# Two pairs of heads in four 64x64 quadrants: products of batch 0 and batch 1 laid out crossed

## The chip, the cores and the metric

The kernel runs on one NeuronCore of a Trainium2 chip. Its engines work side by side and wait for each other by semaphores: TensorE (PE, with its weight loads shown as PEld), VectorE (DVE), ScalarE (ACT), GpSimd (POOL) and SyncE (SP); transfers between the chip's main memory and on-chip memory (SBUF) are made by DMA engines. The results of TensorE stand in PSUM, an accumulator memory that is handed out in banks of 128 partitions x 512 float32. The metric is the time on the device in microseconds (us) of one execution, the median of several runs.

## The reference

q, k and v have shape (8 batches, 8 heads, 576 tokens, 64). Heads 0 to 3 are plain: a token attends to itself and the 31 tokens before it. Heads 4 to 7 are dilated: every fourth token, 32 of them. The result goes through a two-layer network with a squared ReLU.

```python
scores = scale * np.matmul(q, k.transpose(0, 1, 3, 2))
rel = pos[:, None] - pos[None, :]
mask_plain = (rel >= 0) & (rel < window)                                   # window = 32
mask_dil = (rel >= 0) & (rel < window * dilation) & (rel % dilation == 0)  # dilation = 4
attn = np.exp(scores - max); attn = attn / (np.sum(attn, axis=-1, keepdims=True) + 1e-09)
attn_out = np.matmul(attn, v)                                              # (8, 8, 576, 64)
x = attn_out.transpose(0, 2, 1, 3).reshape(8 * 576, 512)
h = np.maximum(x @ w_in, 0.0)                                              # w_in 512 x 2048
out = h * h @ w_out                                                        # w_out 2048 x 512
```

## The kernel before

**Pairs of heads.** Two heads of 64 features share the 128 partitions: pair e = 0, 1 is plain, e = 2, 3 dilated. Head 0 of a pair has the partitions 0 to 63, head 1 has 64 to 127 ("sides"). Keys are cut into blocks of 64. Scores stand with keys on partitions and queries along the row (`pt`, in bfloat16, after the exponential and the mask). The product with v needs, for each block, a weight tile of 128x128 that has head 0's v in the upper left 64x64 and head 1's in the lower right, with zeros elsewhere (`vbd`, and `kbd` likewise for k). Sums over the keys come from the same rows with a tile of ones in the same two corners. So a plain pair's product is a row of matmuls with 128x128 weights that use half of the array.

**Batches.** Batch 0 is the start of the kernel and has its own code (`first_step`); batch 1 goes through `trans`, `halves`, `scores` and `pv`; batches 2 to 7 through `quadrants` (L661), where two pairs are computed at once in four 64x64 quadrants of the array. For this one of the two pairs is "crossed" (`crossed`): its heads' k, v and scores are laid out with the sides exchanged, so that its weights stand in the two corners which the other pair leaves free. Batches 0 and 1 are computed in two parts, part 0 with the first 256 tokens, part 1 with the other 320.

**Steps.** The order of the attention work is written out by hand in the string PROGRAM. A bar separates the FFN's groups: after the group with number g the steps behind the bar number g + 1 are issued. Every engine takes its instructions in the order in which they were issued. In batch 0 a step has a letter, a pair and a part: T and C transpose and copy out, S makes scores, E is the exponential and the mask, P the products, D the sums, L the logarithm of the sums, X the exponential of its negative (so the reciprocal), M the product of both, into `xT`, the FFN's input. Steps of batch 1 begin with 1: q, k (Q, K for part 1) transposes, a (b) scores with exponential and mask, o (p) products, sums, reciprocal and the write to `xT`. A step with an f takes its PSUM from the pool `ps_f`, which the FFN uses too. j copies rows of v of batch 0 into `vbd`, and n zeroes `kbd` for batch 1.

**FFN.** A group computes 2 to 8 matmuls of the first layer (L937, evicted by ACT's ReLU and squared on DVE) or 4 of the second (L979). The first 1024 tokens go through it 256 at a time, the others 512 at a time. The group that first needs part 1 of pairs 0 and 1 of batch 0 comes two groups after P11 and D11.

The lines that matter here: `pv` has the products at L414 and the sums at L416, ACT's L418 and L419, and the write to `xT` on DVE at L429. In `first_step` the same are L851 (P), L867 (D), L874 (L), L877 (X) and L884 (M); masks are at L362 and L824. In batch 0:

```python
P01 D01 L01 X01 M01 P11 D11 L11 X11 M11     # after the fifth FFN group
```

Of the kernel before, what the change touches and what calls it, by code (L numbers as in the profile page):

```python
# [12 lines left out]
RES = 4  # L13
# [9 lines left out]
    "L1:q00123 z y L1:v0dp L1:q10123 w10 T00 C00a T10 C10a B00 B10 w1 S00 E00 B20 W1 S10 E10 N u B30 W1 w1 T20q "  # L23
    "w1 T20k C20v T30 C30v h W1 w1 S20 E20 w1 S30 E30 T21 C21v T31 C31a G20 G30 P00 P10 D00 D10 L00 X00 P20 P30 "
    "D20 D30 L20 X20 M00 j S21 S31 w1+31 M20 E21 E31 G21 G31a | | T01 C01v T11 C11a R P21 P31 D21 D31 S01 S11 L21 "
    "X21 M21 L31 X31 M31 E01 E11 | L2:q00123 L2:q10123 L1:v1dpr | | P01 D01 L01 X01 M01 P11 D11 L11 X11 M11 | | | "
    "| | | | | | | | | m n | | | | | | 1q1 1q3 | 1q2f 1k2f | 1k1a 1v3 | 1a2 | 1v2 1k0a 1q0v | 1o2 | 1a0 1a1 | 1k3 "
    "1o0 1o1f | 1a3 1Q0 | 1K0 1o3 | 1Q1 1K1 | 1Q2 | 1b0 | | 1Q3 1K2 L2:vwp L3:q00123 L3:q10123 L2:vwdr | L2:x | | "
    "| | 1V2 | 1b2 1p0 | 1b1 1V3 1K3 | L3:x | 1p2 1p1f | 1b3 | 2t0 2t1 1p3f | | | L3:Vd0 L4:q00123 L4:q10123 "
    "L3:V1 | | | | | | | | | | L4:x | | f | | | | | | | | | | | | | | | | L4:Vd L5:q10123 L5:q00123 L4:V01 | | | "  # L30
    "| | | | | | | | | | | | | L5:x | L5:Vd L6:q10123 L6:q00123 L5:V01"
)
# [30 lines left out]
def kernel(  # L63
# [9 lines left out]
    nc = tc.nc  # L73
# [100 lines left out]

    def crossed(b: int, e: int):

        return int(b == XB and e in (1, 3) or b >= NATURAL and e == 1 or b >= PAIRED and e == 0)

    def load_v(b: int, parts, which="pdr"):

# [85 lines left out]
    def trans(b: int, e: int, nm: str, part: int, home: str):  # L266

        pool, name = (ps_f, "pf") if "f" in home else (ps_a, "pa")
        ps = pool.tile([P, 1024], bf16, name=name)
        t = staged(b, nm)  # L270
        copy = copier(nm, e, home)
        m0, n, pitch, cuts = MS[part], MN[part], 80, [(t[0 : MT[part], part, :, :], 0, MT[part])]
        pv_ = ps[:, 0 : 4 * pitch].rearrange("p (h c m) -> p h c m", h=2, c=2)
        for hl in range(2):
            for c in range(2):
                for src, c0, w in cuts:
                    nc.tensor.transpose(  # L277
                        pv_[:, hl, c, c0 : c0 + w], src[:, 2 * e + hl, P * c : P * c + P], ident[0:w, 0:w]
                    )
        ready[b, e, nm] = pv_[:, :, :, 0:n], m0, n, copy  # L280
        halves(e, nm, *ready[b, e, nm], (0,) if "l" in home else (0, 1))

    ready = {}

# [1 line left out]
        act = "a" in home or "v" not in home and nm == "q" and e < NE // 2  # L286
        return nc.scalar.copy if act else nc.vector.tensor_copy

    def halves(e: int, nm: str, t, m0: int, n: int, copy, his=(0, 1)):


        for hl in his:
            rows = slice(64 * hl, 64 * hl + 64)
            for jj in range(2):
                src = t[64 * jj : 64 * jj + 64, hl, :, :]
                if nm == "q":
                    copy(
                        qT[rows, e, :, m0 : m0 + n].rearrange("p (c j) m -> p j c m", j=2)[:, jj, :, :], src
                    )
                elif e < NE // 2:  # L300
                    copy(
                        kbd[rows, e, m0 // 16 : (m0 + n) // 16, rows].rearrange(
                            "p i (m c j) -> p j i m c", c=2, j=2)[:, jj, :, :, :],
                        src.rearrange("p c (i m) -> p i m c", m=16),
                    )
                else:
                    x0, x1 = m0 // 64, min((m0 + n) // 64, 2)
                    copy(
                        kbd[rows, e, RES * x0 : RES * x1, rows].rearrange(
                            "p (x c j) m -> p j c x m", c=2, j=2)[:, jj, :, :, :],  # L310
                        src[:, :, 0 : 64 * (x1 - x0)].rearrange("p c (x m) -> p c x m", m=64),
                    )
                    if m0 + n == M:
                        copy(
                            kbd[rows, e, 8, rows].rearrange("p (m c j) -> p j m c", c=2, j=2)[:, jj, :, :],
                            src[:, :, n - 16 : n].rearrange("p c m -> p m c"),
                        )
# [46 lines left out]
            in1=mask[:, off : off + n], op=ALU.mult,  # L364
        )

    def pv(b: int, e: int, part: int, spare=None, name=""):
        dil = e >= NE // 2
        pt, vb = pts[e], vbd[b % 2]
        if spare is None:  # L370
# [20 lines left out]
        else:  # L391
# [9 lines left out]
            for i, r, m0, m1 in () if mms else blocks(b, e, part):  # L401
# [8 lines left out]
                    w = m1 - m0  # L410
                    mms.append((o3[:, r, x0:x1], i, pt[:, c : c + w]))
                c += w
        for x, (oo, i, rh) in enumerate(mms):
            nc.tensor.matmul(oo, vb[:, e, i, :], rh, start=(x == 0), stop=(x == len(mms) - 1), skip_group_check=True)  # L414
        for x, (dd, rh) in enumerate(dms):
            nc.tensor.matmul(dd, ones[:, :], rh, start=(x == 0), stop=(x == len(dms) - 1), skip_group_check=True)  # L416
        rec = r_pool.tile([P, 576], f32, name="rec")
        nc.scalar.activation(rec[:, 0:n], d[:, 0:n], ACT.Ln)  # L418
        nc.scalar.activation(rec[:, 0:n], rec[:, 0:n], ACT.Exp, scale=-1.0)  # L419
# [13 lines left out]
    def step(b: int, code: str):  # L433

        what, e, home = code[0], int(code[1]), code[2:]
        part = int(what in "QKVbp")
        his = (0,) if "l" in home else (1,) if "h" in home else (0, 1)
        if what in "qk" and (b > XB or b == XB and e >= NE // 2):  # L440
            t = (qx if what == "q" else kx)[b % 2]
            halves(e, what, t[:, 2 * e : 2 * e + 2, :, :], 0, M, copier(what, e, home), his)
        elif what in "qQkK" and "h" in home:
            halves(e, what.lower(), *ready[b, e, what.lower()], his)
        elif what == "t":
            trans_both(e)
        elif what in "qQkK":
            trans(b, e, what.lower(), part, home)
        elif what in "vV":
            spread_v(b, e, [part] if b in PARTED else [0, 1])  # L450
        elif what in "ab":
            scores(b, e, part)
        elif "f" in home:
            pv(b, e, part, ps_f, "pf")
        else:
            pv(b, e, part)
# [278 lines left out]
    def first_step(code: str):  # L735
# [56 lines left out]
        elif what == "S":  # L792
# [7 lines left out]
            y = 0  # L800
            for x, (i, r, q0, q1) in enumerate(bl):
                z = (q1 - q0) * (RES if r is None else 1)
                for rows in sides:
                    if dil and i == 8:
                        lhs = k8[rows, e - NE // 2, :]
                    else:
                        k0 = S * e + (M * (i % RES) + 64 * (i // RES) if dil else 64 * i)
                        lhs = xx[0][rows, 1, k0 : k0 + 64]
                    if r is None:
                        to, rhs = byr(ps[rows, y : y + z]), qk0[rows, 0, e, :, q0:q1]  # L810
                    else:
                        to, rhs = ps[rows, y : y + z], qk0[rows, 0, e, r, q0:q1]
                    nc.tensor.matmul(
                        to, lhs, rhs, start=(part == 1 and x == 0), stop=(x == len(bl) - 1), skip_group_check=True
                    )
                y += z
            first["S", e, part] = ps[:, 0:y]
        elif what == "E":
# [3 lines left out]
            if part:  # L822
                mask = (mask_d if dil else mask_p)[:, c : c + ps.shape[1]]
                nc.vector.tensor_tensor(out=to, in0=to, in1=mask, op=ALU.mult)  # L824
        elif what == "P":
            if ("P", *pair) not in first:
                if pair in ((2, 0), (2, 1), (0, 1)):
# [237 lines left out]
    def run(code):  # L1065
# [14 lines left out]
        elif code[0] == "G":  # L1080
            spread_v(0, int(code[1]), [int(code[2])], nc.scalar.copy if code[3:] else nc.vector.tensor_copy)
        elif code == "h":
            for rows in sides:
                nc.vector.tensor_copy(vbd[0][rows, 0:2, 0:4, rows], plain[rows, :, :, :])
        elif code == "j":
            for rows in sides:
                nc.vector.tensor_copy(vbd[0][rows, 2:4, 8, rows], tail[rows, :, :])
        elif code == "n":
            zero_halves(kbd)
        elif code == "f":  # L1090
            nc.sync.dma_start(mask_n[:, :], near_dram.ap())
        elif code[0] in "wW":
            n, _, at = code[1:].partition("+")
            turn(int(n), 512 if code[0] == "w" else 256, [int(x) for x in at])
        elif code[0] in "TCBSEPDXM" or code[0] == "L" and code[2:3] != ":":
            first_step(code)
        elif code[0] != "L":
            step(int(code[0]), code[1:])
        else:
            b, what, part, which = int(code[1]), code[3], code[4:5], code[5:]  # L1100
            if what == "V":
                load_v_rows(b, code[4:] or "d01")
                return
            if what == "q":
                load_qk(b, None if part == "w" else int(part), [int(e) for e in which])
            elif what == "x":
                cross_all(b)
            elif what == "v":
                load_v(b, [0, 1] if part == "w" else [int(part)], which)
            else:  # L1110
                (load_w_in if what == "i" else load_w_out)(int(part))
# [126 lines left out]
```

## Time and profile before

| | |
|---|---|
| median of 3 runs | 299.42 us (298.89 to 299.48) |
| profiled execution | 299.32 us, of which 297.5 us are the span from the first to the last instruction |
| PE busy | 290.4 us, 98% of the span, 3159 matmuls |
| PEld busy | 166.3 us |
| ACT, DVE, POOL busy | 192.0, 168.0, 127.6 us |
| L937 and L979, PE | 128.3 and 129.3 us |
| granted PE clock | 1.00 throughout |

A line of the timeline has the start in us from the beginning of the span, the length in us, the engine, the line in the kernel, the operation, output and inputs, the tile of the array (128*128 or 64*64), shapes, and the number of instructions that were merged into the line. In square brackets stands the idle time of the engine before it, and what ended it. Matmuls overlap in the array, so one that lasts 0.27 us can be followed by the next after 0.11 us. A line of the table of stretches has the stretch, its length, then for each engine the busy time and the number of instructions, the granted clock, the DMA share and GB/s.

### The profile page before, as it was taken

To read this page: it belongs to the slowest core of one execution; us is meant where nothing else is said; L and a number is where in the kernel's file an instruction comes from. 1 tells how busy PE (TensorE), PEld (TensorE's weight loads), DVE (VectorE), ACT (ScalarE), POOL (GpSimd) and SP (SyncE) were. 2 spreads that over 40 slices of the span, in tenths; PEclk is the share of its full clock that TensorE was granted. 3 is DMA by queue.
4 is the path that set the end of the run, shared out by engine and by line. 5 is a ranking of instruction groups with operands and counts; after the bars stand their busy time and mean duration, and the time that the engine had idled before them with its cause. 6 is when DMAs were issued, how large, how long until landed. Compare 5 with 4: busy or idle time off the path is not lost.

```text
span 297.5 us, 7852 instructions
## 1 busy us (share of the span) xinstructions
PE 290.4 (98%) x3159; PEld 166.3 (56%) x3159; DVE 168.0 (56%) x508; ACT 192.0 (65%) x397; POOL 127.6 (43%) x208
## 2 busy tenths in 40 slices
PE   7899999999999999999999999999999999999994
PEld 3589657868755554555455445545554555445443
DVE  2776566967868665686749474957445234004400
ACT  6888568757958665888667667766676567127411
POOL 8579882676584383955783688100000000000000
PEclk9999999999999999999999999999999999999999
DMA  8999999999989999999999499112101200121022
GB/s 126 197 183 215 203 157 223 186 151 169 193 114 185 184 121 190 153 125 175 159 191 151 65 160 186 13 37 73 35 2 36 74 35 0 35 73 35 0 56 88
DMA packets 83124, 35.37 MB, mean 119 GB/s; under 512 B 52624, under 2 KB 78480, under 8 KB 83088
## 3 DMA queue, kind: packets, MB, share of 16 engines
q0 software_dynamic: 48992, 18.40, 54.8%
q1 hardware_dynamic: 33952, 16.38, 27.7%
q8 instruction: 25, 0.41, 0.6%
q10 hardware_dynamic: 144, 0.10, 0.1%
q14 instruction: 11, 0.09, 0.1%
HBM read 37.31 MB, written 9.44 MB: 157 GB/s over the span
## 4 chain that ended last, share of the span: by engine, by line
PE 90%; DMA 5%; ACT 2%; POOL 1%; issue 1%; DVE 1%; ACTq 0%; POOLq 0%
PE pf L937 42%; PE pf L979 40%; DMA w_in<-in_moe_w_in_dram 3%; DMA kb<-in_k_dram 2%; PE po L661 2%; PE pa L661 1%; PE pf L661 1%; POOL qb L171 1%; PE pa L277 1%; PE pd L661 1%; ACT rec L684 0%; ACT pt L698 0%; POOL kb L171 0%; ACT rec L674 0%; PE po L414 0%
## 5 line engine op out<-in xcount | busy, mean ns | idle before, releaser
L937 PE MATMUL pf<-xT,w_in 128*128 128x512 bf16 (+1 forms) x704 | 128.3, 341 | 1.3 <-DMA w_in<-in_moe_w_in_dram 1.3
L979 PE MATMUL pf<-w_out_sb,h2T 128*128 128x512 bf16 (+2 forms) x592 | 129.3, 374 | 0.0
L937 PEld LDWEIGHTS <-w_in 128*128 128x128 bf16 x704 | 77.9, 113 | 48.0 <-DMA w_in<-in_moe_w_in_dram 1.7
L950 ACT ACTIVATE h2T<-pf 128x512 bf16<-128x512 f32 x144 | 83.7, 600 | 29.5 <-PE pf L937 29.3
L951 DVE TENSOR_TENSOR h2T<-h2T 128x512 bf16<-128x512 bf16 x144 | 60.3, 424 | 60.1 <-ACT h2T L950 57.8
L979 PEld LDWEIGHTS <-h2T 128*128 128x128 bf16 x592 | 55.5, 98 | 61.6
L478 POOL DMA_DIRECT2D vbd<-in_v_dram x80 | 43.0, 547 | 24.3 <-DMA qb<-in_q_dram 10.2
L985 ACT COPY osb<-pf 128x512 f32<-128x512 f32 (+1 forms) x34 | 19.5, 573 | 49.7 <-PE pf L979 49.5
L171 POOL DMA_DIRECT2D qb<-in_q_dram x18 | 13.0, 720 | 9.7 <-DMA xx<-qb 7.9
L684 ACT ACTIVATE rec<-rec 128x576 f32<-128x576 f32 x24 | 16.4, 682 | 0.7
L698 ACT ACTIVATE pt<-pa 128x384 bf16<-128x384 f32 (+1 forms) x28 | 12.7, 498 | 6.2 <-DVE xT L689 3.7
L192 POOL DMA_DIRECT2D vbd<-in_v_dram x16 | 10.9, 691 | 9.1 <-DMA kb<-in_k_dram 4.3
L687 DVE TENSOR_TENSOR xT<-po,rec 128x512 bf16<-128x512 f32 x14 | 9.7, 691 | 7.5 <-ACT rec L684 7.2
L171 POOL DMA_DIRECT2D kb<-in_k_dram x18 | 12.7, 706 | 1.7 <-issue 0.7
L465 POOL DMA_DIRECT2D vd<-in_v_dram x20 | 12.0, 616 | 2.9 <-DMA vbd<-in_v_dram 2.9
L470 POOL DMA_DIRECT2D vbd<-in_v_dram x20 | 12.0, 615 | 2.7 <-DMA vbd<-in_v_dram 2.2
L700 DVE TENSOR_TENSOR pt<-pt,mask_n 128x448 bf16<-128x448 bf16 (+1 forms) x20 | 7.1, 373 | 9.5 <-ACT pt L698 9.4
L700 DVE TENSOR_TENSOR pt<-pt,mask_f 128x384 bf16<-128x384 bf16 x24 | 8.4, 355 | 6.0 <-ACT pt L698 5.9
L687 DVE TENSOR_TENSOR xT<-pf,rec 128x512 bf16<-128x512 f32 x10 | 6.9, 691 | 8.5 <-ACT rec L684 8.5
L492 DVE COPY qT<-xx 64x576 bf16<-64x576 bf16 (+1 forms) x30 | 10.8, 360 | 0.6
L661 PEld LDWEIGHTS <-vbd 64*64 64x64 bf16 x288 | 7.6, 107 | 4.2 <-issue 4.2
L698 ACT ACTIVATE pt<-pf 128x448 bf16<-128x448 f32 (+1 forms) x18 | 8.5, 521 | 0.5 <-PE pf L661 0.3
(156 smaller groups left out, 311.8 us busy)
## 6 DMA issues: line engine op xcount, KB each, us to landing
qb<-in_q_dram POOLq DMA_DIRECT2D x7, 320.0 KB, 5.3
kb<-in_k_dram POOLq DMA_DIRECT2D x7, 320.0 KB
vd<-in_v_dram POOLq DMA_DIRECT2D x32, 64.0 KB, 6.1
w_in<-in_moe_w_in_dram POOLq DMA_DIRECT2D x4, 512.0 KB, 8.6
w_out_sb<-in_moe_w_out_dram POOLq DMA_DIRECT2D x4, 512.0 KB, 13.0
out_dram<-osb SPq DMA_DIRECT2D x16, 128.0 KB, 5.3
qb<-in_q_dram POOLq DMA_DIRECT2D x7, 256.0 KB, 7.6
kb<-in_k_dram POOLq DMA_DIRECT2D x7, 256.0 KB
```

Of the source, the lines that this page charges most:

```text
L171: nc.gpsimd.dma_start(t[0:n, part, hs, :], src[b, hs, t0 : t0 + RES * n, :].rearrange("h (p r) d -> p h (r d)", r=RES))
L478: nc.gpsimd.dma_start(v_rows[b % 2][p0 + 16 * r : p0 + 16 * r + 16, e, :, :], v[b, 2 * e + hl, :, :].rearrange("(i m r) d -> r m i d", r=R ...
L661: nc.tensor.matmul(out, lhs, rhs, start=begin, stop=True, skip_group_check=True)
L684: nc.scalar.activation(rec[:, :], rec[:, :], ACT.Exp, scale=-1.0)
L687: nc.vector.tensor_tensor(out=tok[:, :, 16:M], in0=byr(o[:, :]), in1=byr(rec[:, 0:512]), op=ALU.mult)
L698: nc.scalar.activation(pt, sp[b, e][g][:, 0:n], ACT.Exp, scale=SCALE)
L700: nc.vector.tensor_tensor(out=pt, in0=pt, in1=mask, op=ALU.mult)
L937: nc.tensor.matmul(to, w_in_sb[piece][:, kt, c0 : c0 + 509 : 4], rhs, start=(kt == kts[0] and x == 0), stop=(kt == kts[-1] and x == per - ...
L950: nc.scalar.activation(hv, acc[u][:, :].rearrange("p (x n) -> p x n", x=per), ACT.Relu)
L951: nc.vector.tensor_tensor(out=hv, in0=hv, in1=hv, op=ALU.mult)
L979: nc.tensor.matmul(cur[m][:, c0:c1], h2[:, f, P * m : P * m + P], w_out_sb[:, f, c0:c1], start=(f == 0), stop=(f == NF - 1),)
L985: (nc.vector.tensor_copy if last and part == 1 or tk0 == 3 * NT // 2 else nc.scalar.copy)(osb[:, c0:c1], cur[m][:, c0:c1])
```

## The change

Pair 1 of batches 0 and 1 becomes crossed. Its keys are copied to the other columns of `kbd` (batch 1), its scores of part 1 are written to the other partitions (batch 0), its v is loaded to the other sides. Three places then compute two pairs side by side in 64x64 quadrants: the new step Q of batch 0 does P01, D01, P11 and D11 at once; `pv_two` does batch 1's 1o0 and 1o1, and 1p2 and 1p1. Each matmul with 128x128 weights becomes two with 64x64 weights, one for each head, and the instructions of the two pairs are issued in turn, one of each quadrant. PSUM tiles are as before. The former `pv` becomes a generator `products`, so that the instructions behind the products (L, X, M) are issued in the same order as before: first those of the first pair, then those of the second. Since part 0 of batch 0 is still done with uncrossed blocks, and block 3 of pair 1 is used in both parts, j copies that block a second time to the crossed corners, with two more copies. n zeroes pair 1's other corners, so its two instructions become six.

```diff
-X21 M21 L31 X31 M31 E01 E11 | L2:q00123 L2:q10123 L1:v1dpr | | P01 D01 L01 X01 M01 P11 D11 L11 X11 M11 | | |
+X21 M21 L31 X31 M31 E01 E11 | L2:q00123 L2:q10123 L1:v1dpr | | Q01 L01 X01 M01 L11 X11 M11 | | |
...
-1o0 1o1f | 1a3 1Q0 | 1K0 1o3 |
+1+o01 | 1a3 1Q0 | 1K0 1o3 |
...
-1p2 1p1f | 1b3 |
+1+p21 | 1b3 |
@@ crossed
-        return int(b == XB and e in (1, 3) or b >= NATURAL and e == 1 or b >= PAIRED and e == 0)
+        return int(b < XB and e == 1 or b == XB and e in (1, 3) or b >= NATURAL and e == 1 or b >= PAIRED and e == 0)
@@ halves
+            at = sides[hl ^ crossed(b, e)]
-                        kbd[rows, e, m0 // 16 : (m0 + n) // 16, rows].rearrange(
+                        kbd[rows, e, m0 // 16 : (m0 + n) // 16, at].rearrange(
@@ pv
-    def pv(b: int, e: int, part: int, spare=None, name=""):
+    def pv_two(b: int, one, two, part: int):
+        works = products(b, one, part), products(b, two, part, ps_f, "pf")
+        todo = {}
+        for e, work in zip((one, two), works):
+            for s, rows in enumerate(sides):
+                cols = sides[s ^ crossed(b, e)]
+                todo[s, cols.start] = items = []
+                lists = next(work) if s == 0 else lists
+                for kind in lists:
+                    for x, (to, lhs, rh) in enumerate(kind):
+                        items.append((to[cols], lhs[rows, rows], rh[rows], x == 0))
+        while any(todo.values()):
+            for items in todo.values():
+                if items:
+                    to, lhs, rh, begin = items.pop(0)
+                    nc.tensor.matmul(to, lhs, rh, start=begin, stop=True, skip_group_check=True)
+        for work in works:
+            next(work, None)
@@ first_step, scores
-                for rows in sides:
+                for s, rows in enumerate(sides):
+                    at = sides[s ^ (part * crossed(0, e))]
...
-                        to, rhs = byr(ps[rows, y : y + z]), qk0[rows, 0, e, :, q0:q1]
+                        to, rhs = byr(ps[at, y : y + z]), qk0[rows, 0, e, :, q0:q1]
@@ first_step, new
+        elif what == "Q":
+            for e, pools in ((0, ((ps_o, "po"), (ps_d, "pd"))), (1, ((ps_a, "pa"), (ps_a, "pa")))):
+                first["P", e, 1] = od = [pool.tile([P, 512], f32, name=nm) for pool, nm in pools]
+                for s, rows in enumerate(sides):
+                    cols = sides[s ^ crossed(0, e)]
+                    todo[s, cols.start] = items = []
...
+            while any(todo.values()):
+                for items in todo.values():
+                    if items:
+                        to, lhs, rhs, begin = items.pop(0)
+                        nc.tensor.matmul(to, lhs, rhs, start=begin, stop=True, skip_group_check=True)
@@ run
         elif code == "j":
+            for s, rows in enumerate(sides):
+                nc.vector.tensor_copy(vbd[0][rows, 2:4, 8, rows], tail[rows, :, :])
+            for s, rows in enumerate(sides):
+                nc.vector.tensor_copy(vbd[0][rows, 1, 3, sides[1 - s]], plain[sides[1 - s], 1, 3, :])
+        elif code == "n":
+            for es in (slice(0, 1), slice(2, NE)):
+                zero_halves(kbd[:, es])
             for rows in sides:
-                nc.vector.tensor_copy(vbd[0][rows, 2:4, 8, rows], tail[rows, :, :])
-        elif code == "n":
-            zero_halves(kbd)
+                nc.vector.memset(kbd[rows, 1, :, rows], 0.0)
```

## The prediction

> **What bounds the kernel now.** I read the page's busy shares and its chain first, to see which engine the end hangs on; then the timeline of the three places that the change touches, engine by engine; then one later place where four 64x64 quadrants already do the kind of work that the change brings.
>
> ```profile
> PE 290.4 (98%) x3159; PEld 166.3 (56%) x3159; DVE 168.0 (56%) x508; ACT 192.0 (65%) x397; POOL 127.6 (43%) x208
> ...
> PE 90%; DMA 5%; ACT 2%; POOL 1%; issue 1%; DVE 1%; ACTq 0%; POOLq 0%
> ```
>
> PE carries 90% of the chain, so PE time saved is worth its full length unless the stage around it waits for another engine. What stands between is decided in each place. Place A, the last part of batch 0's two plain pairs (P01, D01, P11, D11), first PE, then ACT, then DVE:
>
> ```profile
> 22.20 0.39 PE L851 MATMUL po<-pt,vbd 128*128 128x32 bf16 x6
> 22.43 0.39 PE L867 MATMUL pd<-pt,ones 128*128 128x32 bf16 x6
> ...
> 23.21 5.97 PE L937 MATMUL pf<-xT,w_in 128*128 128x256 bf16 x52
> ```
> ```profile
> 22.85 0.44 ACT L874 ACTIVATE rec<-pd 128x320 f32<-128x320 f32 x1 [0.19 <-PE pd L867]
> ```
> ```profile
> 24.66 0.49 DVE L884 TENSOR_TENSOR xT<-pa,rec 128x320 bf16<-128x320 f32 x1 [0.34 <-ACT rec L877]
> ```
>
> PE spends 22.20 to 23.21 here. ACT stands idle until D01 has ended, then runs L01, X01, L11, X11 without a break (starts at 22.85, 23.32, 23.70, 24.15), and DVE's M11 ends at 24.66 + 0.49 = 25.15. Who needs M11 at once? The FFN group that reads pair 1's new tokens. Two equal stretches of the FFN rows (columns: PE busy with its instructions, PEld busy with its own, clock, DMA) show it:
>
> ```profile
> 25.10:25.19 0.09, 0.09 (x2) 0.00 (x0) 1.00 0.65 125
> 25.21:25.30 0.09, 0.09 (x2) 0.09 (x1) 1.00 1.28 250
> ```
>
> From 25.10 to 25.19 no weight load runs at all: PE has already run out of work and waits for M11. So this stage is limited by D01, then ACT and DVE, not by PE's 1.01 us. The clock is 1.00 in both.
>
> Place B, batch 1's first part (1o0, 1o1f, later 1o3), PE, DVE, ACT:
>
> ```profile
> 47.02 0.32 PE L414 MATMUL po<-pt,vbd 128*128 128x96 bf16 x4
> ...
> 47.37 0.32 PE L414 MATMUL pf<-pt,vbd 128*128 128x96 bf16 x4
> ...
> 49.81 0.28 PE L414 MATMUL po<-pt,vbd 128*128 128x64 bf16 x4
> ```
> ```profile
> 46.62 0.69 DVE L362 TENSOR_TENSOR pt<-pt,mask_p 128x352 bf16<-128x352 bf16 x2
> ...
> 49.45 0.28 DVE L362 TENSOR_TENSOR pt<-pt,mask_d 128x256 bf16<-128x256 bf16 x1
> ```
> ```profile
> 47.53 0.39 ACT L418 ACTIVATE rec<-pd 128x256 f32<-128x256 f32 x1 [0.58 <-PE pd L416]
> ```
>
> The two masks end at 46.62 + 0.34 = 46.96 and at 47.31; pair 0 starts right after the first, pair 1 right after the second. ACT then needs pair 0's sums at 47.53, and the mask of 1a3, behind four ACT steps, ends at 49.73, only 0.08 us before 1o3 starts.
>
> Place C, batch 1's second part, has PE without a gap from 64.32 to 65.26, and nothing waited for. The price of quadrants is read where they run now (PE, the stretch has 68 matmuls):
>
> ```profile
> 83.52:84.22 0.70, 0.70 (x68) 1.00 0.62 39
> ```
> ```profile
> 69.11 1.48 PE L937 MATMUL pf<-xT,w_in 128*128 128x256 bf16 x12
> 70.52 0.34 PE L661 MATMUL pa<-xx 64*64 64x80 bf16 x16
> ...
> 71.00 6.06 PE L937 MATMUL pf<-xT,w_in 128*128 128x256 bf16 x52
> ```
>
> The 68 matmuls are two plain pairs' products and sums; by the code each quadrant streams 832 + 608 = 1440 columns, so a column costs 0.70 / 1440 = 0.486 ns with four quadrants side by side. The twelve FFN matmuls have a pitch of (1.48 - 0.27) / 11 = 0.110, so PE would be free at 70.43 and enters at 70.52: 0.09 for going in. The last quadrant matmul there starts at 70.87 and the FFN at 71.00: coming out takes 0.13 from the last start, of which its own 64 columns are 0.03. A visit takes columns x 0.486 + 0.19 us.
>
> **The change part by part.**
>
> A. Each quadrant has 480 columns of products and 480 of sums: 960 x 0.486 = 0.47, and 0.66 with the switches, against 1.01: PE is back at 22.86, 0.35 earlier. But pair 0's sums, which ended at 22.43 + 0.39 = 22.82, are now spread over the whole visit: the last one starts at 22.20 + 0.09 + 0.44 = 22.73 and takes 0.19, so it ends at 22.92. L01 moves by 0.10, and with it X01, L11, X11 and M11, which are a closed chain. Two FFN groups of 8 x 0.109 cover 1.75 us from PE's return; PE then stands from 24.7 to 25.30 instead of 25.10 to 25.20. The saving is swallowed and A costs +0.10. The bounds: without any overhead per column (0.42 ns, what the FFN's 128x512 matmuls take: 24 of them from 78.25 last 5.34, a pitch of 0.216) +0.04; with the late masks below +0.16.
>
> The two added casts in j (64x64) sit on DVE before M20. The row of the 64x128 casts there has a pitch of 0.24; half of that to all of it for each makes M20 0.24 to 0.48 late, from an end at 14.85 + 0.69 = 15.54. Its reader is the second FFN group, at 15.02 + 8 x 0.109 = 15.89: cover 0.31, so PE loses 0 to 0.17. That is covered at 19.55, where PE waits 0.22 for a weight transfer (w_in); through ACT's copy of T11 it can still reach the mask of E11, which ends at 22.13 (two masks from 21.26 in 0.87) and is now needed at 22.30 by PE's first matmul of pair 1. I take +0.02 of 0 to +0.06. The zeroing in n becomes six instructions instead of two of 1.02 us with the same bytes; DVE's next work is 2.74 us later, so it is hidden, as are the crossed evictions and loads, which keep their number, size and queue on DVE, ACT, SP and POOL.
>
> B. The first matmul of pair 1 is the third in the order and waits for the second mask, with pair 0's remaining items behind it. So the visit runs from 47.37: 352 + 352 columns x 0.486 = 0.34, PE is out at 47.37 + 0.31 + 0.13 = 47.81, against 47.68: +0.13; the 0.15 saved on columns is less than the wait that pair 0 used to fill. Pair 0's sums end one matmul before pair 1's, at about 47.64 + 0.19 = 47.83 instead of 47.17 + 0.32 = 47.49, so L418 starts near 47.87, +0.34. Four ACT steps, a3's exponential and DVE's mask follow with no slack, so the mask ends at 50.05 and 1o3 starts at 50.09 instead of 49.81: B costs +0.28 in all, the 0.13 inside it. Bounds: +0.13 if that chain has slack that I don't see, +0.40 if pair 0's sums end with pair 1's.
>
> C. 1p2 has 1024 columns and 1p1f 960, in items of different width (32, 80, 320 beside 96). Alone the longer one needs 1024 x 0.486 = 0.50; if every round waits for its widest item, 1232 columns, 0.60. In issue order I count about 1136: 0.55, and 0.74 with the switches, against 0.94: -0.20 (bounds -0.25 and -0.15). ACT's L418 comes 0.14 later; b3's mask, four steps on, ends at 67.73 and its reader 1p3f is at 68.61, so this is hidden.
>
> Issue cost is the point where a page speaks against the change. Rows: 68 starts in 0.70 us, 0.010 us each. The Trainium skill, "TensorE: Matmul & The Clock Gate", section "Wait — 56ns, not 53.3ns?", has starts never closer than about 25 ns; by that, A's 48 matmuls would need about 1.2 us (an estimate from that page) and A alone would lose 0.8 at L01. The trace of this kernel disagrees, by its rows of concurrent quadrants, and I go by it.
>
> Sum: +0.10 + 0.02 + 0.28 - 0.20 = +0.20 us on the profiled execution's 299.32 (297.5 span), 299.5; the median of the runs, 299.42, is 0.10 above that execution, so 299.6.
>
> **The rivals.**
>
> Faster: the waits at A and B don't bind, and PE's savings reach the end. That needs M11, or 1a3's mask, to come no later than PE. Then -0.35 - 0.15 - 0.20 = -0.70: 298.7. For it: PE is 90% of the chain. Against it: the empty weight-load stretch at 25.10 and the 0.08 us at 49.73. It decides from the point where M11 ends before 24.7.
>
> Slower by the banks: the two halves of a pair write the same bank of po or pd. If they can't do so at the same time, each visit has half its rate: A's sums +0.47 later, B's +0.34, C +0.55: 299.6 + 1.36 = 301.0. Against it: the visit at 83.52 writes both halves of po and still streams 1440 columns per quadrant in 0.70. "TensorEngine Tiling (Array Packing)" of the Trainium skill, Gotcha 1, says that different row tiles cannot access one bank simultaneously; the trace agrees only if halves in different partitions are no conflict.
>
> Slower at the start: the casts in j delay M20 and the E11 mask by more than the 0.31 and 0.17 that cover them, or ACT's backlog of evictions behind L11 holds FFN buffers at 26 us; each tenth then goes straight to M11. Worth +0.4 to +0.6 over the sum: 300.1. For it: DVE has no gap between 13.5 and 16.2. Against it: the transfer that PE waits for at 19.55.
>
> **How the numbers follow.** About 0.6 us (0.2%) is what a measurement of this kernel tells from no change, as its runs spread from 298.89 to 299.48. Forecast, both waits bind and C gains: 0.73. Faster rival 0.07, banks 0.05, start 0.12, and 0.03 for something unseen, a third of it on the faster side. The forecast's own terms span -0.08 to +0.47 around zero change (0.04 + 0 + 0.13 - 0.25 and 0.16 + 0.06 + 0.40 - 0.15), that is 299.3 to 299.9, and with the runs' spread of 0.3 on both sides 299.0 to 300.2; this also takes in the start rival's near end. Chances: faster 0.08, same 0.73, slower 0.19.
>
> **What would show it.** A: L01 starts near 22.95, M11 ends near 25.25, and the stretch without weight loads before it is 0.5 to 0.6 us long. B: one visit from 47.4 to 47.8, and an idle PE before 1o3. C: 0.74 us instead of 0.94. All shifted by what came before. I am wrong if the FFN after A runs through without a stop, if a quadrant visit costs more than 0.6 ns per column, or if a new wait stands on PE anywhere after 66 us.

## The result, and the profile after

| | before | after |
|---|---|---|
| median of the runs | 299.45 us (298.89 to 308.93, 6 runs) | 302.16 us (301.41 to 303.6, 6 runs) |
| ratio | | 1.009, 95% interval 1.0074 to 1.0106 |
| profiled execution, span | 299.32, 297.5 us | 301.41, 299.3 us |

The change makes the kernel slower by 0.9%, where 299.6 us and no measurable change were forecast. The one run of 308.93 us was in the chip's slower state, and the ratio leaves it out. First the page of the kernel after, its busy time by engine, its DMA queues and its chain:

```profile
PE 289.6 (97%) x3195; PEld 165.8 (55%) x3223; DVE 167.9 (56%) x514; ACT 191.9 (64%) x397; POOL 128.4 (43%) x208
...
q8 instruction: 25, 0.41, 0.6%
...
PE 93%; ACT 3%; issue 2%; DVE 1%; ACTq 0%
```

PE is busy 0.8 us less than before (290.4; a rough figure, since 28 matmuls lack a record beside their weight loads), and the span is 1.8 us longer: PE stands idle somewhere. The queue that brings instructions, q8, looks like nothing, with 25 packets and 0.6%. It turns out to be the line that matters.

Where the time went can be read by one device. The FFN makes the same weight loads in the same order in both kernels, so the start of the n-th one after, less its start before, is what has been lost or won up to there:

```
before   after   shift   what lies between
15.92    16.09   +0.17   M20 late, by the two added casts of j
19.55    19.30   -0.25   the wait for w_in is gone
21.44    21.52   +0.08   a wait for M31 instead
23.21    22.96   -0.25   A, PE's own time
25.20    25.49   +0.29   the wait for M11
47.65    48.09   +0.44   B, the visit
49.94    50.60   +0.66   B, 1o3 waits for its mask
65.24    65.74   +0.51   C
70.99    71.70   +0.70   a pause of 0.2 us inside a quadrant visit at 71.02 to 71.24
72.01    74.00   +1.99   a stop of PE in the middle of an FFN group
84.91    86.65   +1.73   an old wait of 0.38 us at 84.76 is absorbed
293.48  295.23   +1.75   nothing more
```

Place A, timeline of the kernel after, PE, ACT and DVE:

```profile
22.84 0.19 PE L880 MATMUL pa<-pt,ones 64*64 64x64 bf16 x2
22.96 2.04 PE L993 MATMUL pf<-xT,w_in 128*128 128x256 bf16 x17
25.49 0.71 PE L993 MATMUL pf<-xT,w_in 128*128 128x256 bf16 x5 [0.48 <-DVE xT L940]
```
```profile
23.14 0.44 ACT L930 ACTIVATE rec<-pd 128x320 f32<-128x320 f32 x1 [0.30 <-PE pa L880]
```
```profile
24.94 0.49 DVE L940 TENSOR_TENSOR xT<-pa,rec 128x320 bf16<-128x320 f32 x1 [0.34 <-ACT rec L933]
```

The FFN group waits for M11, which ends at 25.43 instead of 25.15. Place B, where the 1o3 that waits for its mask (DVE) is the second half of the cost:

```profile
47.31 0.23 PE L394 MATMUL po<-pt,vbd 64*64 64x96 bf16 x2
47.66 0.23 PE L394 MATMUL pf<-pt,vbd 64*64 64x96 bf16 x2
...
47.95 0.22 PE L394 MATMUL pf<-pt,ones 64*64 64x64 bf16 x2
...
50.48 0.28 PE L374 MATMUL po<-pt,vbd 128*128 128x64 bf16 x4
```
```profile
50.15 0.28 DVE L363 TENSOR_TENSOR pt<-pt,mask_d 128x256 bf16<-128x256 bf16 x1
```

Two matmuls start at 47.31, and the rest of the visit stands behind the second mask until 47.66. The mask of 1a3 ends at 50.43, and 1o3 starts 0.05 later: the chain is as tight as before. Place C has no wait, from the first to the last start:

```profile
65.10 0.20 PE L394 MATMUL po<-pt,vbd 64*64 64x32 bf16 x2
...
65.62 0.19 PE L394 MATMUL pd<-pt,ones 64*64 64x64 bf16 x2
```

The pause at 71.02 to 71.24 is a wait for DVE. A matmul of the visit at 71.0 writes `pa`, which DVE has to copy out first, and PE goes on 0.05 us after that copy's end at 71.18. Before, the copy ended at 70.25, 0.27 ahead of the same matmul. Timelines of after and of before:

```profile
70.73 0.45 DVE L262 COPY qT<-pa 128x576 bf16<-128x576 bf16 x1
```
```profile
69.80 0.45 DVE L262 COPY qT<-pa 128x576 bf16<-128x576 bf16 x1
```

Last the stop, in the chain of the kernel after (start, length, what), then in the timelines of after and of before:

```profile
71.77 1.11 PE pf L993 x9
72.88 1.12 issue
74.00 1.03 PE pf L993 x8
```
```profile
71.70 1.17 PE L993 MATMUL pf<-xT,w_in 128*128 128x256 bf16 x9
74.00 2.21 PE L993 MATMUL pf<-xT,w_in 128*128 128x256 bf16 x17 [1.12 <-issue]
```
```profile
71.00 3.22 PE L937 MATMUL pf<-xT,w_in 128*128 128x256 bf16 x26
```

"issue" says that PE waited for nothing that the profile shows. Before, the same 26 matmuls (9 and 17 after) ran through in 3.22 us from 71.00. The timeline after names no tile, no semaphore and no engine for the gap. The granted clock is 1.00 across it. What does stand there, in the DMA queues of the stretch 71.3 to 72.7 alone, is one packet of the instruction queue:

```profile
q1 hardware_dynamic: 501, 0.12, 196.2%
q0 software_dynamic: 128, 0.01, 23.1%
q8 instruction: 1, 0.02, 5.4%
```

In the stretch 68 to 71.3 that queue has no row at all.

### The profile page after: what moved, and what is told of

Read it like the earlier page. It is cut to its first block, busy times and chain, and to the rows that moved or that the text cites. A ratio compares the mean times of both kernels' runs of the same rounds, so it can differ in the third digit from the quotient of the medians.

```text
span 299.3 us, 7953 instructions
## 1 busy us (share of the span) xinstructions
PE 289.6 (97%) x3195; PEld 165.8 (55%) x3223; DVE 167.9 (56%) x514; ACT 191.9 (64%) x397; POOL 128.4 (43%) x208
## 4 chain that ended last, share of the span: by engine, by line
PE 93%; ACT 3%; issue 2%; DVE 1%; ACTq 0%
PE pf L993 41%; PE pf L1035 40%; PE po L762 2%; PE po L692 2%; PE pf L692 1%; PE pa L692 1%; PE pa L792 1%; PE pd L692 1%; ACT rec L930 1%; DVE xT L940 1%; ACT h2T L1006 1%; ACT rec L933 1%; PE pa L277 1%; PE pf L822 0%; ACT rec L446 0%
## 5 line engine op out<-in xcount | busy, mean ns | idle before, releaser
L1035 PE MATMUL pf<-w_out_sb,h2T 128*128 128x512 bf16 (+2 forms) x571 | 127.3, 373 | 1.6 <-issue 0.8
L509 POOL DMA_DIRECT2D vbd<-in_v_dram x80 | 43.7, 569 | 22.6 <-DMA qb<-in_q_dram 12.0
L1041 ACT COPY osb<-pf 128x512 f32<-128x512 f32 (+1 forms) x34 | 19.5, 574 | 49.5 <-PE pf L1035 46.4
L192 POOL DMA_DIRECT2D vbd<-in_v_dram x16 | 10.9, 692 | 8.1 <-DMA kb<-in_k_dram 2.4
L501 POOL DMA_DIRECT2D vbd<-in_v_dram x20 | 12.1, 623 | 1.2 <-PE pf L993 1.1
L525 DVE COPY kbd<-xx 64x320 bf16<-64x320 bf16 (+3 forms) x32 | 8.4, 263 | 0.6
```

Source lines behind the costliest of these rows:

```text
L509: nc.gpsimd.dma_start(v_rows[b % 2][p0 + 16 * r : p0 + 16 * r + 16, e, :, :], v[b, 2 * e + hl, :, :].rearrange("(i m r) d -> r m i d", r=R ...
L1035: nc.tensor.matmul(cur[m][:, c0:c1], h2[:, f, P * m : P * m + P], w_out_sb[:, f, c0:c1], start=(f == 0), stop=(f == NF - 1),)
L1041: (nc.vector.tensor_copy if last and part == 1 or tk0 == 3 * NT // 2 else nc.scalar.copy)(osb[:, c0:c1], cur[m][:, c0:c1])
```

## The experiments

Theory 1, formed from these rows: PE's instructions come through queue q8 in packets of 16 KB, 25 in the whole run. In the trace of after PE has 3223 weight loads, as many matmuls, and 58 waits and markers of its queue, each an instruction of its own: 6504. 6504 / 25 is 260, and I take 256 for a packet. PE may use up such a block faster than the next one arrives, and then stops. The change adds 64 weight loads and 64 matmuls, 128 PE instructions, and packs them closer. Theory 2: the stop belongs to the dense stretch itself (quadrants, PSUM, transfers), or to its time, and the number of instructions ahead of it is nothing to it.

Tiny matmuls on zeros, whose results nothing reads, shift the block ends without touching the work. The packets' own times, from the DMA records of each trace, stand against PE's weight loads here. "Block end" is the time at which PE passes the 256th instruction, counted through the program (the origin of the count was set once, by the pauses in the first traces, and kept for all kernels); the packet is the next one of q8; then come the last weight load before the next block end and the first one after it.

```
kernel                        block end  packet         last load  next load
before                          68.81    72.40 - 73.67    77.14      77.15
after                           68.02    71.39 - 72.60    72.60      74.00
before + 64 matmuls             68.06    70.67 - 71.59    72.18      73.25
after + 64 matmuls              67.25    70.99 - 72.09    71.44      73.31
batch 1's part alone            75.25    78.15 - 79.89    80.08      81.40
after + 8 matmuls               67.94    70.42 - 71.38    71.62      72.69
after + 9 wide matmuls          68.20    70.31 - 71.25    71.88      72.69
after, sums first               67.36    70.25 - 72.00    71.73      73.31
after + 36 matmuls              65.80    69.33 - 70.23    71.50      71.88
sums first + 30 matmuls         65.58    69.07 - 69.97    71.16      71.39
```

In the seven kernels from the second row to the eighth that stop for over 0.8 us, PE goes on 1.22 to 1.66 us after the packet's end. The count itself agrees with the blocks. From the program's start, waits of PE's queue included, 1985 or 1986 instructions stand ahead of the pause in all eight kernels that have it at 71 to 74 us, although up to 128 instructions were added ahead of it. In batch 1's part it is 2241, which is 256 more. Before used its block up only at 77.14, 3.5 us after the packet; none of its blocks between 60 and 90 us lasted less than 6.5 us, while the block of after that began at 68.02 was used up in 4.6.

**The kernel before with 64 matmuls more.** At the start ten idle matmuls of 512 columns are replaced by 74 of 64 columns: 128 PE instructions more, the change itself absent.

```diff
@@ turn (before)
+        if n == 10:
+            n, cols, rhs = 10 + 64, 64, idle[:, 0:64]
```

> The kernel before, with the ten idle 128x512 matmuls of the first 4.7 us cut into 74 of 64 columns: 64 more weight loads and 64 more matmuls, 128 PE instructions, as many as the change adds, in a stretch where PE waits for the first transfers. Nothing else is changed. Theory 1 (PE's instructions are fetched in blocks of 16 KB, and the 128 extra instructions move the end of a block into the fast stretch from 67.8 to 71.7 us): a stop of PE of about 1 us without a wait near 72 to 74 us, as in the changed kernel, and 300.5 to 300.8 us. Theory 2 (the 1.3 us stop at 74 us comes from the change's own timing, or from transfers in the way): no such stop, 299.4 us.

Measured: 300.74 us (299.58 to 301.82), ratio 1.0039 (1.0017 to 1.0061). A stop appears that the kernel before does not have, in its timeline:

```profile
71.61 0.85 PE L939 MATMUL pf<-xT,w_in 128*128 128x256 bf16 x6
73.25 0.92 PE L939 MATMUL pf<-xT,w_in 128*128 128x256 bf16 x7 [0.80 <-DVE pt L700]
```

The profile puts it down to a DVE step, which ends at 73.18. That step is not the cause: in the kernel before the same matmul starts at 71.68, 0.9 us ahead of the same step's end (72.57). The weight loads stop at 72.18 and go on 1.66 us after the packet. A second, of 0.55 us, follows at 79.96. Shift against before in the profiled executions: +0.60 at 25 us, +1.57 after the first stop, +2.12 after the second. So the stop comes without a single quadrant of the change: it isn't a property of the new code.

**The kernel after with the same 64.**

> The changed kernel with the same 64 more idle matmuls at the start: 256 instructions more than before, a whole block of 16 KB if an instruction has 64 bytes. Theory 1: block ends lie in the same places as before, the stop at 74 us is gone, and the rest of the change's loss is left: about 0.5 us over before, 299.9 us. Theory 2: the stop stays, 302 us.

Measured: 302.79 us (301.54 to 303.87), ratio 1.0104 (1.0058 to 1.0151). The stop is still there, one group earlier:

```profile
71.47 0.30 PE L374 MATMUL pf<-pt,ones 128*128 128x320 bf16 x1
73.31 0.26 PE L374 MATMUL pf<-pt,ones 128*128 128x128 bf16 x2 [1.55 <-issue]
```

My expectation that 128 + 128 = 256 instructions bring the old block ends back did not hold. The change had also made the instructions ahead of this block end denser: this block was used up in 4.2 us (67.25 to 71.44), so the old place is no longer a safe one. The run also lost 1.84 us by 19.5 us, behind a wait for M20 there, so its time says little beyond the place of the stop.

**Batch 1's part alone, batch 0's part alone.** In the first batch 0 keeps P01 D01 ... P11 D11 and j has no added casts; in the second batch 1 keeps 1o0 1o1f and 1p2 1p1f and the zeroing of n is the old one.

```diff
@@ batch 1's part alone (against after)
-... | Q01 L01 X01 M01 L11 X11 M11 | ...
+... | P01 D01 L01 X01 M01 P11 D11 L11 X11 M11 | ...
@@ batch 0's part alone (against after)
-1+o01 | ... | 1+p21 |
+1o0 1o1f | ... | 1p2 1p1f |
```

> The change in batch 1 alone (1+o01, 1+p21; batch 0 as before): 80 PE instructions more. By the parts measured between the two traces B costs +0.37 (0.15 at the visit, 0.22 at 1o3) and C gives back 0.15: 299.65 without a fetch stop. Theory 1: the stop depends on where 80 instructions put the block ends; theory 2, if the stop comes from C's visit: it stays, about 301.

> The change in batch 0 alone (Q01 with the crossed scores and the two extra copies in j; batch 1 as before): 48 PE instructions more. By the two traces the last step of A (M11's wait) leaves +0.29 at 25.5 us: 299.7 if nothing else stops. The stop of 0.65 us before the FFN group that reads M11 should be there, with the first saving of 0.35 in front of it. Theory 2, if the stop at 74 us comes from the crossed layout of batch 1 or C: it is absent here.

Measured: batch 1's part 301.05 us (299.35 to 303.31), ratio 1.0065 (1.0031 to 1.0099); batch 0's part 300.03 us (299.47 to 300.99), ratio 1.0015 (1.0000 to 1.0031). Timeline of batch 1's part, then of batch 0's:

```profile
78.78 1.89 PE L1035 MATMUL pf<-w_out_sb,h2T 128*128 128x512 bf16 x7
81.41 0.82 PE L1035 MATMUL pf<-w_out_sb,h2T 128*128 128x512 bf16 x3 [0.74 <-DVE xT L718]
```
```profile
25.56 0.71 PE L993 MATMUL pf<-xT,w_in 128*128 128x256 bf16 x5 [0.47 <-DVE xT L940]
```

With 80 instructions added instead of 128, batch 1's part stops too, but at 80 us instead of 73, again 1.51 us after a packet's end (79.89); the DVE step that the profile names cannot be what it waited for, since before the same weight load starts 1.2 us ahead of that step's end (79.76 and 80.91). With 48 added, batch 0's part has no stop between 60 and 90 us. The small terms come out as in the kernel after: B +0.15 and then +0.22, C -0.16; batch 0's part has the wait for M11 and is 0.36 late at 25.6, 0.24 at the end. The two ratios together (0.65 and 0.15%) are near that of the change (0.90%), but the stop is not in the same place: it moves with the number of instructions ahead of it, and does not belong to C's visit, which batch 1's part has as well.

**36 matmuls where PE waits anyway, and 8.** They stand ahead of the FFN group that waits for M11.

```diff
-... Q01 L01 X01 M01 L11 X11 M11 | | | "
+... Q01 L01 X01 M01 L11 X11 M11 | | s36 | "     (s8 in the other)
+    def small(n: int):
+        to = first["W"] = first.get("W") or ps_o.tile([P, 512], f32, name="po")
+        for _ in range(n):
+            nc.tensor.matmul(to[:, 0:16], idle[:, 0:P], idle[:, 0:16], start=True, stop=True, skip_group_check=True)
```

> The kernel after the change, with 36 further matmuls on zeros (128x16, 72 TensorE instructions with their weight loads) put where TensorE waits about 0.65 us for the mask product M11 at 24.8 to 25.5 us; their results are used by nothing, and all else is as after. Theory 1 (instruction supply): TensorE's instructions come in blocks of 256, a new one is usable about 5.9 us after the one before the last was used up, and the dense stretch from 64 to 74 us used one up in about 4.5 us; 72 more instructions ahead of it move the block ends so that this stretch is shared among two blocks otherwise. It expects the stop of 1.3 us at 72.6 to 74.0 us at 0.1 us or nothing, 0.2 to 0.3 us of the added work showing at 25 us, and so about 300.4 to 300.9 us in the profiled execution against 301.4. Theory 2 (the stop belongs to the dense stretch itself: transfers, PSUM or the quadrants): the stop stays at 1.2 to 1.5 us at the same place, and the time is 301.6 to 302.4.

> As the run with 36 added matmuls, but with 8 (16 instructions), which fit inside the wait at 25 us and cost nothing there. Theory 1 has the block ends move the wrong way: a stop of 1.7 to 2.1 us (both stops near 72 us added up) in place of 1.3, and 301.8 to 302.4 us in the profiled execution. Theory 2: 1.2 to 1.5 us as after the change, 301.4.

Measured: with 36, 300.80 us (300.54 to 301.47), ratio 1.0039 (1.0014 to 1.0064); with 8, 301.49 us (301.21 to 303.27), ratio 1.0080 (1.0050 to 1.0111). Timelines, with 36 and with 8:

```profile
24.84 1.05 PE L769 MATMUL po<-kbd 128*128 128x16 bf16 x36
...
72.24 3.99 PE L999 MATMUL pf<-xT,w_in 128*128 128x256 bf16 x33
```
```profile
71.61 0.30 PE L999 MATMUL pf<-xT,w_in 128*128 128x256 bf16 x1
72.69 3.52 PE L999 MATMUL pf<-xT,w_in 128*128 128x256 bf16 x29 [0.78 <-issue]
```

Idle work added makes the kernel faster: with the 36 the ratio falls from 1.0090 to 1.0039. The FFN group runs through, and what is left at the block end is a pause of 0.38 us between two weight loads, up to 71.88. With 8 the stop stays. Theory 1 is right on which of the two kernels stops and wrong on a size: it had 1.7 to 2.1 us for the 8, and the shift over the stop is 0.95, also less than the 1.2 to 1.5 of theory 2. The packet came sooner, 2.5 us after the block end instead of 3.4. The 5.9 us that I had taken as fixed are not: from one block end to PE's going on the seven kernels took 4.5 to 6.2.

**The control: as long, but 18 instructions instead of 72.** Both fillers take about 1.0 us at the same place, so the dense stretch starts equally late: B's visit ends at 48.47 with the 36 and 48.46 here.

```diff
-... | | s36 | "
+... | | s9 | "
-            nc.tensor.matmul(to[:, 0:16], idle[:, 0:P], idle[:, 0:16], start=True, stop=True, skip_group_check=True)
+            nc.tensor.matmul(to[:, 0:256], idle[:, 0:P], idle[:, 0:256], start=True, stop=True, skip_group_check=True)
```

> The control to the run with 36 added matmuls: the kernel after the change with 9 idle matmuls of 128x256 at the same place, which take the same TensorE time as the 36 of 128x16 (about 1.0 us, two thirds of it inside the wait for M11), but are 18 instructions instead of 72. Theory 1 (instruction supply) expects the stop near 73 us to stay, at 0.9 to 2 us, since 18 instructions move the block ends about as little as the 16 of the run with 8 matmuls did; profiled execution 301.3 to 302.6 us. If it was the later start of the dense stretch, by 0.3 to 0.4 us, and not the number of instructions, that let the run with 36 matmuls pass without a stop, this run passes too: no stop over 0.2 us near 73 us, 300.4 to 300.9.

Measured: 301.73 us (301.22 to 302.03), ratio 1.0077 (1.0060 to 1.0094).

```profile
24.76 1.15 PE L769 MATMUL po<-kbd 128*128 128x256 bf16 x9
...
72.69 3.52 PE L999 MATMUL pf<-xT,w_in 128*128 128x256 bf16 x29 [0.73 <-ACT pt L729]
```

PE's time, place and lateness are those of the 36, and the stop is back: the shift goes from 0.85 to 1.68 us, 0.83, a little under the 0.9 that was the least expected. The medians say the same, 300.80 and 301.73. So the number of instructions decides, and not the time at which the stretch begins. The profile again names a wrong releaser, an ACT step: before, the same matmul starts 0.8 us ahead of that step's end (71.00 and 71.80).

**Sums first.** This one is for the wait at A: in the new groups the matmuls with the ones go ahead of the products.

```diff
@@ pv_two
-                for kind in lists:
+                for kind in lists[::-1]:
@@ Q
-                    for y, (to, ones_) in enumerate(zip(od, (False, True))):
+                    for y, (to, ones_) in enumerate(zip(od[::-1], (True, False))):
```

> The kernel after the change with the row sums' matmuls (the ones) issued ahead of the products in each of the new quadrant groups, so that the reciprocal on VectorE or ScalarE starts before the products are done; no instruction more or less. If the lateness of M11 (0.65 us of wait at 25 us, +0.29 against before) and of the second visit of batch 1 (+0.22) comes by way of the sums, the wait at 25 us falls by 0.15 to 0.3 us and the visit at 50 us by 0 to 0.2; the stop near 73 us stays at 1.2 to 1.5 us, since no block end moves; profiled execution 300.9 to 301.3. If the lateness comes from VectorE's queue instead, both waits stay within 0.1 us of those after the change.

Measured: 301.63 us (300.93 to 302.21), ratio 1.0069 (1.0047 to 1.0091). ACT, then PE:

```profile
22.63 0.44 ACT L930 ACTIVATE rec<-pd 128x320 f32<-128x320 f32 x1
```
```profile
24.98 1.25 PE L993 MATMUL pf<-xT,w_in 128*128 128x256 bf16 x10 [0.18 <-DVE xT L940]
...
73.31 2.86 PE L993 MATMUL pf<-xT,w_in 128*128 128x256 bf16 x23 [1.31 <-issue]
```

L01 starts 0.51 us earlier than after the change, 0.21 of it because the group ahead of A was earlier, and the idle time before the FFN group falls from 0.48 to 0.18: the late sums were what made M11 late. B's visit loses 0.16 instead of 0.15, but what follows up to 54 us only 0.06 instead of 0.22. At 65 us this kernel is 0.15 us ahead of the kernel before. The stop, where no instruction was added or taken, stays at 1.46, and a second, of 0.56, follows at 79.75, 1.45 us after a packet's end. That second stop was not expected, and the profiled execution, 301.44 us, lies above the 300.9 to 301.3 that were.

**Sums first, and 12 and 18 idle matmuls in two waits.**

```diff
+... | s12 | Q01 L01 X01 M01 L11 X11 M11 | | s18 | ...      (and sums first)
```

> Sums first as in the run before, and 12 and 18 idle matmuls (60 TensorE instructions) put in the two places near 21 and 25 us where TensorE waits. Theory 1: the block ends move so that the stop near 73 us is at most 0.15 us; with the waits at 25 us shorter by the sums this gives 299.4 to 300.2 us in the profiled execution, within 0.3% of the kernel before. Theory 2: the stop stays, 300.9 to 301.5.

Measured: 300.18 us (299.38 to 301.50, 12 runs), ratio 1.0023 (1.0006 to 1.0039). The group runs through:

```profile
71.69 4.53 PE L999 MATMUL pf<-xT,w_in 128*128 128x256 bf16 x38
```

The idle matmuls remove the stop; what is left are a pause of 0.2 us at the block end at 71.39 and, in this execution, a wait of 0.75 us for a transfer of v at 78.43. With them the profiled execution takes 300.49 us, more than the 299.4 to 300.2 expected. This is the best version that keeps all of the change, and it is no faster than the kernel before.

**Batch 0's part alone, sums first.** The edit is the hunk of Q of "sums first", on batch 0's part alone. It adds 48 PE instructions, as batch 0's part does; the 16 in the expectation is wrong.

> Only batch 0's part of the change (its last part in quadrants, its second pair crossed; batch 1 as in the kernel before), with the sums' matmuls ahead of the products there. Theory 1: 16 instructions more than before leave no block end that stops TensorE between 60 and 90 us; the wait for M11 falls from 0.63 us (batch 0's part alone) to 0.25 to 0.4, and the profiled execution is 299.1 to 299.5 us, a ratio of 0.998 to 1.001 against the kernel before. If the sums do not lead M11, the wait stays at 0.6 and the time at 299.5 to 300.0.

Measured: 299.86 us (298.90 to 301.96, 12 runs), ratio 1.0023 (0.9996 to 1.0049).

```profile
25.03 1.14 PE L993 MATMUL pf<-xT,w_in 128*128 128x256 bf16 x9 [0.17 <-DVE xT L940]
```

Its profiled execution, 298.90, is 0.44 us below that of the kernel before by the weight loads, but the other runs go up to 301.96, and the median ratio is above the 0.998 to 1.001 expected, so nothing can be said for it from the times.

## Why the prediction was wrong

By its own steps, each against the shifts of the profiled executions:

- **A, the chain from D01 to M11: right.** M31 ends 0.16 late and M11 0.28, so A's own share is +0.12 where +0.10 was predicted. PE's return 0.35 earlier was predicted; it came 0.33 earlier (+0.08 to -0.25). The stand of PE before M11 was 0.65 beyond the usual pitch, 0.6 predicted. Sums first confirms that the chain hangs on the sums.
- **j's two casts: the mechanism right, the cover wrong.** M20's lateness cost PE 0.17, the upper bound. I let the wait for w_in at 19.55 absorb it. After, PE did not wait for w_in, arrived 0.25 earlier and waited for M31 instead, because ACT and DVE had carried the 0.16 on. In batch 1's part alone, without these casts, M31 is 0.02 early. The term was +0.02 and is 0.16. It is a marginal one: with the sums first the casts are still there, M20 ends at 15.83 instead of 16.04, and M31 is 0.03 early.
- **B: right in kind, 0.37 instead of 0.28.** The visit lost 0.15 (0.13 predicted) and 1o3 another 0.22 (0.15 predicted).
- **C: -0.15 instead of -0.20**, its bound. What follows C was not hidden, as I had it: ACT's L418 (L446 after) starts at 65.86 instead of 65.01, 0.16 more than PE's own lateness of 0.69 there (0.14 predicted). The mask and DVE's copies follow in order, and at 71.0 PE waits 0.19 for the last of them. I had looked only at the mask's own reader, 1p3f.
- **The step that failed is the sum.** A + j + B + C makes +0.20 predicted and +0.51 measured at 65.74, and by that alone the execution would have stayed inside the range. The sum then treats PE's later work as merely moved by what came before. It has no term for the instructions themselves: 128 more of them, so that a block of 256 was used up in 4.6 us, where the shortest of before between 60 and 90 us took 6.5. The price is 1.29 us at 72.6 and the largest single item. The paragraph on issue cost asked how close together starts may lie, and found 0.010 us in the rows, which A bears out (48 starts from 22.37 to 22.84); it did not ask whether instructions arrive at such a rate. What would make it wrong was named ("a new wait stands on PE anywhere after 66 us"), but only 0.03 was left for it. The four small terms together, +0.51, came out just above the +0.47 that the forecast had as their upper bound; it is the 0.3 added for the runs' spread that would have kept them inside the range.

The bridge from 297.7 (the span before plus 0.20) to 299.3: 1.29 the stop, 0.19 the pause at 71.0, 0.31 the small terms, and 0.26 back at 84.9 where an old wait was absorbed. That is +1.53 of 1.6. The execution has about 0.3 more than before outside the span.

A page of the Trainium skill bears on this, "Runtime: NRT & Kernel Launch", section "Instruction fetch mechanics". It says that the instructions are refilled in blocks of 16 KiB, 256 instructions, by a DMA queue of the engine's own, and that crossing a block's end is mostly hidden. The first half agrees with 25 packets and 0.41 MB here. The second fails here where a block is used up before the next one has come, which took 4.5 to 6.2 us in the seven kernels: the block of after at 68.02 took 4.6, and PE stopped.

The rivals: neither the start nor the banks was it. The two halves in one bank stream at the predicted rate (A's visit and C's show no half rate), and PE's waits at A and B did bind, so the faster one fell too.

What stays open: what the packet waits for, 2.1 to 3.7 us between a block end and its start in the ten rows of the table (it is no constant: in the kernel before one packet starts at 216.82, 2 us ahead of the block end that the count has at 218.82); and why five runs of after that have no trace lie 0.5 to 2.2 us above the profiled one. That a stop so dependent on a packet's arrival differs from run to run would fit, but no trace shows it. The bridge above is for the profiled execution alone. That the stop also costs the runs without a trace is seen from the medians: with the 36 idle matmuls the median is 300.80 instead of 302.16.

## What to carry to other kernels

Splitting a 128x128 matmul into two of 64x64, as here, doubles its instructions; count PE's instructions per stretch, and where 256 of them would run in less than about 6 us, ask whether the block ends fall so that PE stops. It need not stop: by the same count a block of the kernel before lasts 5.2 us (218.82 to 224.01) without a pause, with a packet just ahead of it. A gap of PE marked "issue", or a wait put down to an engine that had long been done, beside a single packet of the instruction queue 1.2 to 1.7 us earlier, is how that looks; a few idle matmuls in an existing wait, or another order of dense and sparse work, move it. In a group that feeds a reciprocal, issue the sums ahead of the products.

## What the runs showed of the hardware

Blocks of 256 PE instructions came in 16 KB packets that took 0.9 to 1.9 us each. Where PE had used up its block, it went on 1.2 to 1.7 us after the packet's end. The profile has no name for such a wait: it writes "issue", or names an engine or a transfer that came last before it.

A block also ends ahead of the FFN's first weight load near 15 us. In all ten kernels without the 64 matmuls at the start 449 instructions stand before that load, 6 x 256 fewer than 1985, and it starts 1.3 to 1.6 us after a packet of the instruction queue (before: 13.65, with 8: 13.97, batch 0's part: 13.96). Timeline of before, of after with 8, and of batch 0's part:

```profile
15.02 0.84 PE L937 MATMUL pf<-xT,w_in 128*128 128x256 bf16 x6 [1.03 <-DMA w_in<-in_moe_w_in_dram]
```
```profile
15.27 0.52 PE L999 MATMUL pf<-xT,w_in 128*128 128x256 bf16 x3 [1.21 <-DVE vbd L1151]
```
```profile
15.26 0.52 PE L993 MATMUL pf<-xT,w_in 128*128 128x256 bf16 x3 [1.21 <-DVE vbd L1145]
```

How much of this idle time the block cost differs. The group needs w_in and M00's product. Before, w_in landed at 14.84, and at 19.55 PE started 0.04 us after another landing of w_in; so w_in did hold PE for most of the 1.03 us, and the block for some 0.14. In batch 0's part w_in had landed at 13.85 and M00 had ended at 14.43, and PE started 0.8 us later; the DVE copy that the profile names there writes `vbd`, which this matmul does not read (its inputs are xT and w_in).
